# Layer 2's split operands in seven fixed places, each at its own distance mod 256 bytes from the weights

## The chip, the cores and the metric

The kernel runs on one core of a Trainium2 chip. The metric is device time in microseconds (us), less is better. A core has TensorE (PE in the views; PEld is its weight load), VectorE (DVE), ScalarE (ACT), GpSimd (POOL) and SyncE (SP), which here issues every DMA. SBUF holds operands, PSUM (eight banks of 512 float32 columns) the results of matmuls.

## What is computed

Attention over 4 x 8 heads of 576 tokens with a compressive memory, and behind it two feed-forward layers on 2304 tokens of 512 features. The change is in the second.

```
def _moe2_ref(x, w_in, w_out, alpha):
    h = x @ w_in                                     # 2304x512 @ 512x2048
    g = np.maximum(h, 0.0) + alpha * np.minimum(h, 0.0)
    return (g @ w_out).astype(np.float32)            # 2304x2048 @ 2048x512
```

All is float32. The matmuls of both layers are done in float32r: each operand is cut into a high part (a cast to float32r) and a low part (what the cast left over), and a product is three matmuls: high x high, high x low, low x high.

## The kernel before

`build()` records every operation with its engine, its estimated time and what it reads and writes, and `Plan.order()` then simulates the engines and writes one order of instructions for each. So the order on an engine is fixed when the program is built, and an instruction that waits holds up all that stand behind it on its engine.

**Layer 1** runs blocks of 512 tokens (the first) and 256 tokens (the others; in one of them the second matmul has 258 columns). Its operands are cut from `xr` and `gr` by `cut()`, which adds `SKEW` = 48 words (192 bytes) where a block has fewer than 512 columns and nothing where it has 512.

**Layer 2** saves matmuls by forming sums of quarters of its matrices: a 2 x 2 block product takes seven products P = 1 to 7 in place of eight. `hidden()` makes h: for each of 3 blocks b of 384 token columns it loads the four quarters of layer 1's result into `spare` (`inputs`), forms the sums by `sub`, and lets `split` write the parts of each of the seven operands into a place: ACT casts 768 columns (L1198), then DVE subtracts (L1199). `TURN` = 1, 5, 6, 3, 2, 7, 4 is the order of the operands. Then follow 8 groups of seven products. A product (`product`, L1241 to L1243) is six matmuls of 128 x 128 weights and 384 columns. Its bank is then read by `copy_out` (ACT, L1253) or `join` (DVE, L1256), and `leak` (ACT L1267, DVE L1268) makes the activation, which goes to DRAM.

`output()` makes the second matmul of layer 2. For each b and each P in the order 4, 1, 5, 6, 3, 7, 2 there are four steps m: `sub` where a sum is wanted, `split` into the next place of a ring of three, and 12 matmuls of 384 columns (L1373 to L1375).

**Places.** A place holds four runs of 384 columns: high k = 0, high k = 1, low k = 0, low k = 1, here back to back (1536 words). There are eight: five in `poolr`, two in `xr`, one in `gr`, and operand P of block b goes to

```
def XP(P, b):
    return room_for[(7 * b + TURN.index(P)) % 8]
```

so each block starts one place further back, and the first operand of a block finds a place that the block before it doesn't use. The ring of `output()` is the upper place of `xr`, `gr`, the lower place of `xr`; in the last block these held operand 1, operand 5 and operand 4. In the built program `poolr`, `xr`, `gr` and every weight tile `wp` begin at the same address mod 256 bytes, and a 128-column weight is 512 bytes long. So all 2016 matmuls of layer 2 read columns that begin at distance 0 mod 256 bytes from their weights; layer 1's begin at distance 192 where they have 256 or 258 columns, and at 0 where they have 512.

## Time and profile before

| | |
|---|---|
| median of 3 runs (lowest, highest) | 937.96 us (936.33, 938.33) |
| the profiled execution | 939.22 us, of which the span of the profile is 937.2 us |
| PE busy | 921.1 us (98%), 7164 matmuls |
| DVE, ACT busy | 717.4 us (77%), 604.6 us (65%) |
| granted TensorE clock | 1.000 |
| layer 2's first matmul, between those of layer 1 | 569.8 us in the span |
| layer 2, hidden() | to 757.6 us |
| layer 2, output() | from 757.6 us to the end |

The time of an execution is the span and 2.0 us that lie around it. Pitch is used below for the time from the start of one matmul to the start of the next: the length that a row gives for a matmul contains its way through the array, which overlaps the next, and says little about the rate.

### The profile page before, as it was taken

The page shows a single profiled execution, that of the slowest core. Times are in us where ns is not written, and L with a number is a line of the kernel's source. Part 1 is how long each engine was busy: PE and PEld are TensorE (multiplying, and loading weights), DVE is VectorE, ACT ScalarE, POOL GpSimd, SP SyncE. Part 2 cuts the span into 40 slices and gives each one's busy share as a digit, 9 for nine tenths or more (in the row PEclk, how much of TensorE's full clock was granted, in tenths as well). Part 3 has the DMA queues.
Part 4 walks back from the last instruction along what each step waited for, and adds up shares of the span by engine and source line. Part 5 has one row for each costly group of instructions (what it writes and reads, how often), then busy time and mean ns, then how long its engine had stood idle before and what let it go on. Part 6 is the DMA issues. An engine that isn't in the chain of part 4 may idle for free.

```text
span 937.2 us, 19293 instructions
## 1 busy us (share of the span) xinstructions
PE 921.1 (98%) x7164; PEld 845.2 (90%) x7164; DVE 717.4 (77%) x1636; ACT 604.6 (65%) x1413; POOL 5.3 (1%) x29
## 2 busy tenths in 40 slices
PE   7999999999999999999999999999999999999998
PEld 5677777688888888999999999999999999999998
DVE  6999998857777776647778767859568889786874
ACT  7887757767888888744544479748457665454452
POOL 1000000000000000000000000000000000000000
PEclk9999999999999999999999999999999999999999
DMA  4358955466766575567967746635348793725301
GB/s 158 98 144 254 284 180 166 124 139 128 183 146 148 121 168 109 90 185 253 323 228 281 257 156 218 210 111 165 115 133 271 231 306 117 238 68 163 107 1 68
DMA packets 154094, 160.43 MB, mean 171 GB/s; under 512 B 86928, under 2 KB 127888, under 8 KB 154000
## 3 DMA queue, kind: packets, MB, share of 16 engines
q1 hardware_dynamic: 154000, 159.20, 57.4%
q8 instruction: 56, 0.92, 0.4%
q14 instruction: 38, 0.31, 0.1%
HBM read 92.84 MB, written 46.66 MB: 149 GB/s over the span
## 4 chain that ended last, share of the span: by engine, by line
PE 83%; DVE 10%; ACT 3%; issue 2%; DMA 2%; SPq 0%; DVEq 0%; ACTq 0%
PE yb L962 6%; PE yb L964 6%; PE hb L928 6%; PE yb L963 6%; PE hb L929 6%; PE hb L930 6%; PE yb L1373 3%; PE sp L1374 3%; PE yb L1374 3%; PE sp L1373 3%; PE yb L1375 3%; PE sp L1375 3%; PE yb L1241 3%; PE yb L1243 3%; PE yb L1242 3%; PE sp L1243 2%
## 5 line engine op out<-in xcount | busy, mean ns | idle before, releaser
L962 PE MATMUL yb<-gr,wt 128*128 128x256 f32 (+2 forms) x512 | 154.5, 302 | 0.8 <-ACT gr L943 0.5
L928 PE MATMUL hb<-xr,wt 128*128 128x256 f32 (+1 forms) x512 | 152.9, 299 | 2.3 <-ACT gt L941 2.2
L964 PE MATMUL yb<-gr,wt 128*128 128x256 f32 (+2 forms) x512 | 151.5, 296 | 0.8 <-DVE gr L944 0.5
L930 PE MATMUL hb<-xr,wt 128*128 128x256 f32 (+1 forms) x512 | 149.7, 292 | 0.3 <-DVE wt L894 0.3
L929 PE MATMUL hb<-xr,wt 128*128 128x256 f32 (+1 forms) x512 | 149.7, 292 | 0.0
L941 ACT ACTIVATE gt<-hb 128x256 f32<-128x256 f32 (+1 forms) x128 | 52.3, 408 | 91.4 <-PE hb L930 76.9
L928 PEld LDWEIGHTS hb<-xr,wt 128*128 128x128 f32 x512 | 96.3, 188 | 11.3 <-issue 4.4
L962 PEld LDWEIGHTS yb<-gr,wt 128*128 128x128 f32 x512 | 96.3, 188 | 9.2 <-issue 3.7
L944 DVE TENSOR_TENSOR gr<-gt,gr 128x256 fp32r<-128x256 f32 (+1 forms) x128 | 58.3, 456 | 58.9 <-ACT gr L943 56.7
L964 PEld LDWEIGHTS yb<-gr,wt 128*128 128x128 f32 x512 | 96.9, 189 | 5.7 <-DVE gr L944 2.8
L930 PEld LDWEIGHTS hb<-xr,wt 128*128 128x128 f32 x512 | 96.7, 189 | 3.5 <-DVE wt L894 0.9
L929 PEld LDWEIGHTS hb<-xr,wt 128*128 128x128 f32 x512 | 96.3, 188 | 2.1
L963 PE MATMUL yb<-gr,wt 128*128 128x256 f32 (+2 forms) x320 | 93.8, 293 | 0.0
L963 PEld LDWEIGHTS yb<-gr,wt 128*128 128x128 f32 x320 | 60.3, 188 | 1.2
L943 ACT CAST gr<-gt 128x256 fp32r<-128x256 f32 (+1 forms) x128 | 55.3, 432 | 6.8 <-PE yb L963 4.4
L942 ACT ACTIVATE gt<-gt 128x256 f32<-128x256 f32 (+1 forms) x128 | 56.9, 445 | 2.8
L963 PE MATMUL yb<-gr,wu 128*128 128x256 f32 (+2 forms) x192 | 56.3, 293 | 0.0
L1198 ACT CAST xr<-spare 128x768 fp32r<-128x768 f32 x37 | 30.9, 836 | 26.6 <-PE sp L1374 10.1
L1267 ACT ACTIVATE waste<-poolx 128x384 f32<-128x384 f32 x48 | 25.2, 526 | 29.2 <-DVE poolx L1256 28.5
L1199 DVE TENSOR_TENSOR xr<-spare,xr 128x768 fp32r<-128x768 f32 x37 | 35.3, 955 | 9.6 <-ACT xr L1198 9.4
L963 PEld LDWEIGHTS yb<-gr,wu 128*128 128x128 f32 x192 | 36.1, 188 | 0.8
L1112 DVE TENSOR_TENSOR wp<-poolx,wp 128x768 fp32r<-128x768 f32 (+1 forms) x32 | 25.9, 822 | 8.9 <-ACT wp L1110 8.1
(505 smaller groups left out, 2570.2 us busy)
## 6 DMA issues: line engine op xcount, KB each, us to landing
g<-poolx SPq DMA_DIRECT2D x96, 192.0 KB, 1.9
poolu<-g SPq DMA_DIRECT2D x30, 384.0 KB, 4.2
room<-wout SPq DMA_DIRECT2D x14, 512.0 KB, 4.1
room<-win SPq DMA_DIRECT2D x13, 512.0 KB, 3.9
pool<-win SPq DMA_DIRECT2D x12, 512.0 KB, 4.6
pool<-wout SPq DMA_DIRECT2D x12, 512.0 KB, 5.0
spare<-y SPq DMA_DIRECT2D x12, 384.0 KB, 3.7
spare<-g SPq DMA_DIRECT2D x12, 384.0 KB, 3.6
```

The source lines that it names most:

```text
L928: T.matmul(H_, W_h, X_h, start=(d == 0), stop=False)
L929: T.matmul(H_, W_h, X_l, start=False, stop=False)
L930: T.matmul(H_, W_l, X_h, start=False, stop=(d == KD - 1))
L942: op("ACT", t_act(n), lambda: A.activation(out=t_, in_=t_, func=AF.Square), w=[tk], prio=-1)
L943: op("ACT", t_act(n), lambda: A.copy(out=G_h, in_=t_), r=[tk], w=[("gh", gj)], prio=-1)
L944: op("DVE", t_dve(n), lambda: V.tensor_tensor(out=G_l, in0=t_, in1=G_h.bitcast(F32), op=ALU.subtract), r=[tk, ("gh", gj)], w=[("gl", gj)], ...
L962: T.matmul(Y, W_h, G_h, start=first, stop=False, skip_group_check=True)
L963: T.matmul(Y, W_l, G_h, start=False, stop=False, skip_group_check=True)
L964: T.matmul(Y, W_h, G_l, start=False, stop=False, skip_group_check=True)
L1373: T.matmul(o, W_h, G_h, start=(m == e == 0 and P in (1, 2, 4, 5)), stop=False, skip_group_check=True)
L1374: T.matmul(o, W_l, G_h, start=False, stop=False, skip_group_check=True)
L1375: T.matmul(o, W_h, G_l, start=False, stop=False, skip_group_check=True)
```

## The change

- There are seven places, and operand P keeps the same one in every block: 1, 5, 6 and 3 in `poolr`, 2 and 7 in `xr`, 4 in `gr`.
- `LAY` gives each place its own start, and a gap of 64 words stands between the high and the low parts. Distances from the weights, mod 256 bytes: operand 1 at 16, operand 5 at 240, operand 6 at 64, operand 3 at 192, operand 4 at 0. In the two places in `xr` the four runs lie at 0, 32, 32, 0 (operand 2) and 0, 224, 224, 0 (operand 7), so that the six matmuls of a product read 0, 32, 0, 32, 0, 32.
- The ring of `output()` is the two places of `xr` and then `gr`. The three matmuls of a weight pair there are put in the order of `product`: high x high, high x low, low x high.
- The loads into `poolu` (the memory of `poolr`) wait for the last products 1, 5, 6, 3 in place of 6, 3, 2, 7.
- In `xr` the runs of a part are no longer contiguous, so the cast and the subtraction there have the shape 2 x 384 for 768.

```diff
--- before.py
+++ after.py
@@ -19,7 +19,9 @@
-NS, NTH = 384, NT // 2
+NS = 384
+LAY = [(4, 384, 836, 384), (60, 384, 892, 384), (16, 384, 848, 384), (48, 384, 880, 384), (0, 392, 840, 440), (0, 440, 888, 392)]
+NTH = NT // 2
...
@@ -1126,8 +1128,9 @@
-            def __init__(self, region, c0, n):
+            def __init__(self, region, c0, n, lay=None):
                 self.region, self.c0, self.n = region, c0, n
+                self.lay = lay or (0, NS, 2 * NS, NS)
...
@@ -1180,12 +1183,12 @@
-        room_for = [Buf("poolr", 4 * NS * i, 4 * NS) for i in range(5)]
-        room_for = room_for[0:4] + [Buf("xr", 0, 4 * NS)] + room_for[4:] + [Buf("xr", 4 * NS, 4 * NS), Buf("gr", 0, 4 * NS)]
+        room_for = [Buf("poolr", 1920 * i, 1664, LAY[i]) for i in range(4)] + [
+            Buf("xr", 2048 * i, 1664, LAY[4 + i]) for i in range(2)] + [Buf("gr", 0, 4 * NS)]
         TURN = (1, 5, 6, 3, 2, 7, 4)
 
         def XP(P, b):
-            return room_for[(7 * b + TURN.index(P)) % 8]
+            return room_for[TURN.index(P)]
...
@@ -1195,10 +1198,20 @@
         def split(src, dst, prio):
-            act(dst, t_act(2 * NS), lambda: A.copy(out=see(dst, F32R, 0, 2 * NS), in_=see(src)), r=src.keys, prio=prio)
+            def raw():
+                return see(src).rearrange("p (k n) -> p k n", k=2)
+
+            act(dst, t_act(2 * NS), lambda: A.copy(out=two(dst, 0), in_=raw()), r=src.keys, prio=prio)
             op("DVE", t_dve(2 * NS), lambda: V.tensor_tensor(
-                out=see(dst, F32R, 2 * NS, 2 * NS), in0=see(src), in1=see(dst, F32, 0, 2 * NS), op=ALU.subtract),
-               r=src.keys, w=dst.keys, prio=prio)
+                out=two(dst, 1), in0=raw(), in1=two(dst, 0).bitcast(F32), op=ALU.subtract), r=src.keys, w=dst.keys, prio=prio)
+
+        def two(buf, lo):
+            a, step = buf.lay[2 * lo:2 * lo + 2]
+            return see(buf, F32R, a, 2 * step).rearrange("p (k n) -> p k n", k=2)[:, :, 0:NS]
+
+        def one_of(buf, lo, k):
+            a, step = buf.lay[2 * lo:2 * lo + 2]
+            return see(buf, F32R, a + step * k, NS)
...
@@ -1235,7 +1248,7 @@
-                    X_h, X_l = (see(XP(P, b), F32R, 2 * NS * lo + NS * k, NS) for lo in range(2))
+                    X_h, X_l = (one_of(XP(P, b), lo, k) for lo in range(2))
...
@@ -1327,7 +1340,7 @@
-            ring = [room_for[6], room_for[7], room_for[4]]
+            ring = [room_for[4], room_for[5], room_for[6]]
...
@@ -1343,7 +1356,7 @@
-                                [("end", P) for P in (6, 3, 2, 7)] if U[q][m].region == "poolu" else []), eng="SP", bytes_=1024 * NS)
+                                [("end", P) for P in (1, 5, 6, 3)] if U[q][m].region == "poolu" else []), eng="SP", bytes_=1024 * NS)
...
@@ -1366,13 +1379,13 @@
-                                    G_h, G_l = (see(dst, F32R, 2 * NS * lo + NS * e, NS) for lo in range(2))
+                                    G_h, G_l = (one_of(dst, lo, e) for lo in range(2))
...
                                         T.matmul(o, W_h, G_h, start=(m == e == 0 and P in (1, 2, 4, 5)), stop=False, skip_group_check=True)
+                                        T.matmul(o, W_h, G_l, start=False, stop=False, skip_group_check=True)
                                         T.matmul(o, W_l, G_h, start=False, stop=False, skip_group_check=True)
-                                        T.matmul(o, W_h, G_l, start=False, stop=False, skip_group_check=True)
```

**First place: the change of block in `hidden()`, on DVE.** These are the operands of block 1 while the last products of block 0 run. `poolr`, `xr` and `gr` are places, `spare` the quarters, `poolx` the sum or h, `wasteN`, `gr2`, `gt` the parts that `join` adds. In the changed program the lines are a few higher: L1205 is L1199 (`split`), L1217 is L1204 (`sub`), L1269 is L1256 (`join`), L1281 is L1268 (`leak`), L1114 is L1112 (weights). Before:

```order
L1199 TENSOR_TENSOR poolr_6986<-poolx_76,poolr_6986 128x768
L1204 TENSOR_TENSOR poolx_76<-poolx_76,spare_99 128x768
L1268 SCALAR_TENSOR_TENSOR poolx_76<-poolx_76,alm_98,sp0_106 128x384
L1199 TENSOR_TENSOR poolr_6986<-poolx_76,poolr_6986 128x768
L1204 TENSOR_TENSOR poolx_76<-spare_99,poolx_76 128x768
L1199 TENSOR_TENSOR poolr_6986<-spare_99,poolr_6986 128x768
L1199 TENSOR_TENSOR xr_77<-spare_99,xr_77 128x768
L1199 TENSOR_TENSOR poolr_6986<-poolx_76,poolr_6986 128x768
L1199 TENSOR_TENSOR poolr_6986<-spare_99,poolr_6986 128x768
L1256 TENSOR_TENSOR poolx_76<-yb1_102,waste1_7330 128x384
```

With the change:

```order
L1205 TENSOR_TENSOR poolr_6986<-spare_99,poolr_6986 128x768
L1205 TENSOR_TENSOR poolr_6986<-poolx_76,poolr_6986 128x768
L1217 TENSOR_TENSOR poolx_76<-poolx_76,spare_99 128x768
L1281 SCALAR_TENSOR_TENSOR poolx_76<-poolx_76,alm_98,sp0_106 128x384
L1269 TENSOR_TENSOR poolx_76<-yb1_102,waste1_7329 128x384
L1205 TENSOR_TENSOR poolr_6986<-poolx_76,poolr_6986 128x768
L1217 TENSOR_TENSOR poolx_76<-spare_99,poolx_76 128x768
L1205 TENSOR_TENSOR xr_77<-spare_99,xr_77 128x2x384 x2
L1205 TENSOR_TENSOR poolr_6986<-poolx_76,poolr_6986 128x768
L1281 SCALAR_TENSOR_TENSOR poolx_76<-waste3_7350,alm_98,poolx_76 128x384
L1269 TENSOR_TENSOR poolx_76<-yb2_103,waste0_7298 128x384
```

The subtraction for operand 1 of block 1 (`poolr<-spare`), done long ahead before, now stands first in this stretch. That for operand 4 (before the last but one row, `poolr<-spare`) has moved behind these rows, and a `join` of the last group stands between those of operands 5 and 6. On PE, product 2 now stands ahead of products 6 and 3 in the first group of block 1; before, the order there was 1, 5, 6, 3, 2.

**Second place: the change from `hidden()` to `output()`, on DVE.** PE's order is the same before and after: the last product 7, the first output step (m = 0), the last product 4 (`gr` now), then m = 1. Before:

```order
L1199 TENSOR_TENSOR xr_77<-spare_99,xr_77 128x768
L1199 TENSOR_TENSOR gr_78<-spare_99,gr_78 128x768
L1268 SCALAR_TENSOR_TENSOR poolx_76<-poolx_76,alm_98,hb_105 128x384
L1112 TENSOR_TENSOR wp13_7257<-poolx_76,wp13_7257 128x3x256
L1256 TENSOR_TENSOR poolx_76<-yb1_102,waste1_7330 128x384
L1112 TENSOR_TENSOR wp14_7334<-waste5_7188,wp14_7334 128x2x256
L1256 TENSOR_TENSOR poolx_76<-yb2_103,waste0_7298 128x384
L1268 SCALAR_TENSOR_TENSOR poolx_76<-waste3_7358,alm_98,poolx_76 128x384
L1256 TENSOR_TENSOR poolx_76<-yb0_101,waste2_7310 128x384
L1268 SCALAR_TENSOR_TENSOR poolx_76<-poolx_76,alm_98 128x384
L1112 TENSOR_TENSOR wp14_7334<-waste4_7093,wp14_7334 128x2x256
```

With the change:

```order
L1269 TENSOR_TENSOR poolx_76<-yb1_102,waste1_7329 128x384
L1114 TENSOR_TENSOR wp14_7309<-waste5_7178,wp14_7309 128x2x256
L1269 TENSOR_TENSOR poolx_76<-yb2_103,waste0_7298 128x384
L1281 SCALAR_TENSOR_TENSOR poolx_76<-waste3_7350,alm_98,poolx_76 128x384
L1205 TENSOR_TENSOR xr_77<-spare_99,xr_77 128x2x384
L1281 SCALAR_TENSOR_TENSOR poolx_76<-poolx_76,alm_98 128x384
L1205 TENSOR_TENSOR xr_77<-spare_99,xr_77 128x2x384
L1269 TENSOR_TENSOR poolx_76<-yb0_101,waste2_7318 128x384
L1114 TENSOR_TENSOR wp14_7309<-waste4_7093,wp14_7309 128x2x256
L1281 SCALAR_TENSOR_TENSOR poolx_76<-waste3_7350,alm_98,poolx_76 128x384
L1205 TENSOR_TENSOR xr_77<-spare_99,xr_77 128x2x384
L1205 TENSOR_TENSOR gr_78<-spare_99,gr_78 128x768
```

Before, the operands of m = 0 and m = 1 (`xr<-spare`, `gr<-spare`) stand eight and seven rows ahead of the `join` of the last product 7 (`yb0`). Now those two (`xr<-spare` twice) stand three rows and one row ahead of it, since their places are those of operands 2 and 7, whose last products have just been issued. On PE the last product 2 writes `yb2`, product 7 `yb0`, and the first output steps `yb2` and `yb3`.

## Rows read from the trace of the kernel before

**Rows 1.** Page: busy us of each engine (share of the span) x instructions.

```profile
PE 921.1 (98%) x7164; PEld 845.2 (90%) x7164; DVE 717.4 (77%) x1636; ACT 604.6 (65%) x1413; POOL 5.3 (1%) x29
```

**Rows 2.** Windows, three stretches of layer 2: stretch, its us, busy us (instructions), clock.

```profile
569.00:600.00 31.00, 31.00 (x223) 30.59 (x222) 25.82 (x40) 27.24 (x58) 0.00 (x0) 1.00 0.66 213
600.00:757.00 157.00, 157.00 (x907) 156.88 (x906) 118.31 (x200) 100.52 (x201) 0.00 (x0) 1.00 0.54 177
757.00:937.00 180.00, 176.66 (x1019) 176.15 (x1017) 135.83 (x163) 81.63 (x112) 0.00 (x0) 1.00 0.40 130
```

**Rows 3.** Timeline of PE, hidden(): start us, length us, instruction; 384 columns, distance 0.

```profile
600.45 0.33 PE L1241 MATMUL yb<-poolr,wp 128*128 128x384 f32 x1
...
603.57 0.33 PE L1241 MATMUL yb<-poolr,wp 128*128 128x384 f32 x1
```

**Rows 4.** Timeline of PE, layer 1's first block: 512 columns, distance 0.

```profile
121.12 0.39 PE L964 MATMUL yb<-gr,wt 128*128 128x512 f32 x1
...
122.48 0.39 PE L964 MATMUL yb<-gr,wt 128*128 128x512 f32 x1
```

**Rows 5.** Timeline of PE, layer 1: 256 columns, distance 192, a quick stretch.

```profile
429.70 0.28 PE L928 MATMUL hb<-xr,wt 128*128 128x256 f32 x1
...
431.06 0.28 PE L962 MATMUL yb<-gr,wt 128*128 128x256 f32 x1
```

**Rows 6.** Timeline of PE, layer 1: 256 columns, distance 192, a slow stretch.

```profile
469.99 0.28 PE L962 MATMUL yb<-gr,wt 128*128 128x256 f32 x1
...
471.40 0.28 PE L928 MATMUL hb<-xr,wt 128*128 128x256 f32 x1
```

**Rows 7.** Timeline of PE, layer 1: 258 columns, distance 192, then 256.

```profile
515.53 0.28 PE L962 MATMUL yb<-gr,wt 128*128 128x258 f32 x1
...
516.97 0.28 PE L928 MATMUL hb<-xr,wt 128*128 128x256 f32 x1
```

**Rows 8.** Timeline of PE at the change from hidden() to output().

```profile
756.53 0.33 PE L1241 MATMUL yb<-poolr,wp 128*128 128x384 f32 x1
...
757.61 0.44 PE L1373 MATMUL yb<-xr,wp 128*128 128x384 f32 x1
757.89 0.33 PE L1374 MATMUL yb<-xr,wp 128*128 128x384 f32 x1
...
759.82 0.33 PE L1241 MATMUL yb<-xr,wp 128*128 128x384 f32 x1
```

**Rows 9.** Timeline of DVE there.

```profile
752.66 0.95 DVE L1199 TENSOR_TENSOR xr<-spare,xr 128x768 fp32r<-128x768 f32 x1
753.57 0.96 DVE L1199 TENSOR_TENSOR gr<-spare,gr 128x768 fp32r<-128x768 f32 x1
...
757.01 0.55 DVE L1256 TENSOR_TENSOR poolx<-yb,waste 128x384 f32<-128x384 f32 x1
757.48 0.60 DVE L1268 SCALAR_TENSOR_TENSOR poolx<-waste,alm,poolx 128x384 f32<-128x384 f32 x1
758.00 0.55 DVE L1256 TENSOR_TENSOR poolx<-yb,waste 128x384 f32<-128x384 f32 x1
```

**Rows 10.** Timeline of ACT there.

```profile
756.52 0.53 ACT L1267 ACTIVATE waste<-poolx 128x384 f32<-128x384 f32 x1 [0.59 <-DVE poolx L1256]
...
759.85 0.84 ACT L1198 CAST xr<-spare 128x768 fp32r<-128x768 f32 x1 [0.68 <-PE yb L1374]
```

**Rows 11.** Timeline of DVE at the first change of block.

```profile
635.87 0.96 DVE L1199 TENSOR_TENSOR poolr<-poolx,poolr 128x768 fp32r<-128x768 f32 x1
...
638.72 0.96 DVE L1199 TENSOR_TENSOR poolr<-poolx,poolr 128x768 fp32r<-128x768 f32 x1 [0.38 <-ACT poolr L1198]
...
642.33 0.95 DVE L1199 TENSOR_TENSOR poolr<-poolx,poolr 128x768 fp32r<-128x768 f32 x1
```

**Rows 12.** Timeline of PE there: the first matmul of product 3.

```profile
644.13 0.33 PE L1241 MATMUL sp<-poolr,wp 128*128 128x384 f32 x1
```

**Rows 13.** Waits of PE in layer 2, from the line of output's first matmul.

```profile
  DVE poolx L1256: 0.2, 1
```

## The prediction

> **What bounds the kernel now.** I read the page first: PE is busy 98% of the span, the other engines 77% and less [rows 1]. That share says little about PE's rate, so I went on to layer 2 by windows: from 600 to 757 us PE starts 907 matmuls of 384 columns in 157.00 us, 173.1 ns each, with the granted clock at 1.00, which is the upper level of 2.4 GHz [rows 2]. Nothing is waited for there, and DVE and ACT have a quarter of the stretch and more to spare. So layer 2 lasts as long as the pitch of its matmuls says, and the questions are whether the new places change the pitch, and whether the new order makes PE wait.
>
> The pitch comes from two starts in PE's timeline and the number of matmuls between them. Layer 2: 18 matmuls in 3.12 us, 173.3 ns [rows 3]. Its 384 columns at 2.4 GHz take 160.0, so 13.3 ns, or 32 cycles, are lost on each. In layer 1's first block, at distance 0 too, 6 matmuls of 512 columns take 1.36 us, 226.7 ns, and lose 13.3 again [rows 4]. In its other blocks, at distance 192, 12 matmuls of 256 columns take 1.36 us, 113.3 ns, and lose 6.7, or 16 cycles [rows 5]. But in other stretches the same matmuls take 117.5 ns (1.41 us for 12) and lose 10.8 [rows 6]. With 258 columns it is 120.0 (1.44 us for 12): two columns more cost 6.7 ns more than the quick stretch, not 0.8 [rows 7]. The reader is to see that the losses differ by steps of some 16 cycles, the time of 16 columns, which are 64 bytes; that distance 0 always loses two steps and distance 192 one, or one to two; and that no row has 384 columns at any distance but 0.
>
> **What the change costs and gives.** 2016 matmuls are concerned: 24 x 6 = 144 for each operand of hidden(), and 84 steps x 12 = 1008 in output(), a third of them in each place of the ring. So operands 1, 5, 6 and 3 have 144 each, the two places in xr 480 each, gr 480. Those in gr stay at distance 0 and keep 173.3 ns [rows 3].
>
> Operand 3 (distance 192, 144 matmuls). The nearest rows are layer 1's. By the quick stretch 6.7 ns less for each, 0.96 us; by the slow one 13.3 - 10.8 = 2.5 ns, 0.36 us [rows 5, 6]. I take the middle, -0.6 us; the bounds are -0.96 and 0.
>
> Operand 6 (distance 64, 144 matmuls). Nothing has this distance; it is 64 bytes from 0 and 128 from 192. I take the nearer, no change. Bounds: one step either way, -0.96 to +0.96 us.
>
> Operands 1 and 5 (distances 16 and 240, 288 matmuls). Nearest is 0: no change taken. One step either way is -1.9 to +1.9 us.
>
> The two places in xr (960 matmuls). Half of their reads begin at 0, half at 32 or 224. Nearest is 0 for both, so no change is taken. Bounds: a step for the shifted half, 480 x 6.7 ns = 3.2 us either way, and 6.4 us down if the alternation takes a step from every one of them. This is the largest unknown of the sum.
>
> The order of the three matmuls in output() costs nothing by itself: as many weights are loaded as before, and PEld is busy beside PE in either order.
>
> The change from hidden() to output(). Before, the operands of m = 0 and m = 1 are finished at 753.61 and 754.53, four and three us ahead of output's first matmul at 757.61 [rows 9, 8]. What that matmul waited for was the join of the last product 2, which frees its bank and ends at 757.56 [rows 9, 13]: 0.05 us from DVE to PE. Now m = 0 goes to the place of operand 2, whose last product ends where product 7 begins, at 756.53 [rows 8]. A cast that waits for PE starts at once (759.85, after a step that ends at 759.82 [rows 10, 8]). ACT has the leak's first half ahead of it, 756.52 to 757.05 [rows 10]; the cast of 0.84 us then ends near 757.85. On DVE the join and the leak stand ahead, to 758.08, and what follows them starts at 758.00, since neighbours overlap by 0.08 [rows 9]. The subtraction of 0.95 us [rows 9] ends at 758.95, and PE starts at 759.0 in place of 757.61: **+1.4 us**. Queued behind this wait on PE is product 4, which would be ready; behind the subtraction on DVE are a leak, the subtraction for m = 1 (from some 759.4 to 760.35) and the join that frees product 4's bank (to some 760.8). Product 4 starts when m = 0 ends, at 759.0 + 2.08 = 761.1, so this second delay is covered, by 0.3 us. The bounds of the step: 0.9 us, if ACT's leak slips behind the cast and DVE's too, and 2.0 us, if the cover of 0.3 fails by as much again.
>
> The two changes of block. Before, operand 5's subtraction starts at 635.87 and operand 3's ends at 643.28, 0.85 us ahead of product 3 at 644.13 [rows 11, 12]. Now operand 1's subtraction (0.9 us of DVE from start to start where two follow each other) and a join (0.47) come in between [rows 9], 1.4 us; but product 3 stands one product later (6 x 173.3 ns, 1.04 us), and DVE waited 0.38 us for ACT in that stretch, which the new work can fill [rows 11]. What is left of the 0.85 is 0.5 to 0.9 us; product 2, now third, has less, some 0.2 to 0.6. I take nothing, and 0.5 us for each of the two changes as the upper bound. If this cover is gone, PE waits us for us.
>
> The first products, between layer 1's last matmuls (569 to 600 us, PE busy 31.00 of 31.00 us [rows 2]), are re-ordered, because operands 7 and 4 now wait for xr and gr to be left by layer 1. Others stand in for them: nothing taken, 0.3 us either way. The 2 x 384 shape of the cast and the subtraction in xr is on engines with time to spare: nothing. The loads into poolu may start two products earlier, and PE waits for none of them: nothing.
>
> Sum: -0.6 + 1.4 = +0.8 us. The profiled execution took 939.22 us, 1.26 over the median of the runs, so it goes to 940.0 and the median from 937.96 to **938.8 us**.
>
> **The rivals.** *The distance decides, and any that isn't 0 is good (faster).* For it: distance 192 loses a step less than distance 0 [rows 5, 3]. All 1536 matmuls away from gr then gain 6.7 ns, 10.2 us: 937.96 - 10.2 + 1.4 = 929.1 us. With the slow stretch's 2.5 ns it is 3.8 us, 935.5. Against it: the rows that differ in distance differ in columns too, and half of the 960 still start at 0.
>
> *A read that begins inside a 64-byte run costs a step (slower).* For it: the 258 columns, which reach two columns into another run and pay for 16 [rows 7, 5]. A start at 16, 32, 224 or 240 makes 384 columns touch 25 runs in place of 24. That holds for 288 + 480 = 768 matmuls: +5.1 us, with the +0.8 of my sum 943.9 us. It decides once some 165 reads more pay a step than save one, 1.1 us beyond my sum. Against it: in a slow stretch 256 columns pay 117.5 ns, and 258 only 2.5 more [rows 6, 7].
>
> *Distances do nothing.* The loss would belong to the columns alone: 13.3 ns with 384 and 512, 6.7 to 10.8 with 256 [rows 3 to 6]. Only the wait is left: 937.96 + 1.4 = 939.4 us. This is also what the Trainium skill says (TensorE: Matmul & The Clock Gate, the section "Step-by-step: what each phase is for"): PE reads the moving operand and the next weights through two independent ports, and loading the one takes no bandwidth from the other. No row here sets it against the same columns at another distance. The same page (the section "Back-to-back issue gap") gives columns / 2.4 + 2.5 ns, 162.5 for 384, as the gap; the trace differs, 173.3. If the new places brought that gap, 1536 x 10.8 ns would go, 16.6 us, to 922.8 by an estimate from that page.
>
> **How the numbers follow.** A measurement here can tell about 0.2%, 1.9 us, from no change: 936.1 to 939.8 counts as same. Chances: my sum 0.31; distances do nothing 0.14; good, in whole or in part, 0.28; the step for a broken run, in whole or in part, 0.27. My sum's own range is 937.2 to 940.2. It and "nothing" (0.45) lie in the middle with about 0.06 over 939.8 and 0.02 under 936.1: same 0.37. Faster 0.28 + 0.02 = 0.30; slower 0.27 + 0.06 = 0.33. The range reaches into both outer cases, 930.0 to 943.5, and leaves out the best of the one and the worst of the other.
>
> **What would show it.** In the changed kernel's timeline of PE, the starts of the products of operands 1, 5, 6, 3, 2, 7 and 4 give the pitch of each place by itself: 173.3 everywhere but 166.7 to 171 for operand 3 is my case; 173.3 everywhere is "nothing"; 166.7 in most is the first rival; 180 in places 16 and 240 and in half the reads of xr is the second. Output's first matmul must start 1.4 us later against the last product 7, with a subtraction (DVE, L1205) named as what ended the wait. I am wrong above all if the 960 alternating matmuls have a pitch of their own, in either direction.

## The result and the profile after

The changed kernel takes 943.84 us in the median of 4 runs (942.81 to 945.65), the kernel before 937.35 beside it: 1.0071 times as long, with a 95% interval from 1.0052 to 1.0091. It is slower by 6.5 us, where 0.8 was forecast. Its profiled execution took 945.65 us, with a span of 943.3, 6.1 more than before.

PE's line of the page, against [rows 1]:

```profile
PE 924.3 (98%) x7164; PEld 845.9 (90%) x7164; DVE 717.2 (76%) x1636; ACT 604.9 (64%) x1413; POOL 5.3 (1%) x29
```

The same 98% again. The first two windows of [rows 2]:

```profile
569.00:600.00 31.00, 29.25 (x205) 28.12 (x205) 22.45 (x34) 25.31 (x53) 0.00 (x0) 1.00 0.70 213
600.00:757.00 157.00, 156.80 (x898) 156.01 (x897) 117.16 (x199) 98.58 (x197) 0.00 (x0) 1.00 0.53 173
```

Two things are to be seen. From 569 to 600 us PE, which never stood still before, is idle for 1.75 us. From 600 to 757 it is idle for 0.20 us only, yet starts 898 matmuls where it started 907, at the same granted clock: the pitch is longer.

**The waits.** PE's waits between 565 and 600 us (line waited at, what ended it, us, times, longest):

```profile
PE sp L1254 <- DVE poolx L1269: 0.8, 1, 0.8
...
PE yb L966 <- DVE gr L946: 0.5, 1, 0.5
...
PE yb L1254 <- DVE poolx L996: 0.4, 1, 0.4
```

Before, this view shows no wait of PE there. L966 is layer 1 (L964 before); in PE's timeline its step with `gr` now waits for its own operand, since no product of layer 2 stands ahead of it to fill the time:

```profile
577.19 0.28 PE L965 MATMUL yb<-gr,wt 128*128 128x256 f32 x1
577.98 0.38 PE L966 MATMUL yb<-gr,wt 128*128 128x256 f32 x1 [0.52 <-DVE gr L946]
```

Which products filled that time can be read from PE's timeline before. The two `sp` rows are the first matmuls of product 6 and product 7, the third row is layer 1's last:

```profile
577.29 0.34 PE L1241 MATMUL sp<-poolr,wp 128*128 128x384 f32 x1
...
584.99 0.33 PE L1241 MATMUL sp<-poolr,wp 128*128 128x384 f32 x1
...
588.63 0.28 PE L964 MATMUL yb<-gr,wt 128*128 128x256 f32 x1
```

With the change the same three come in this order:

```profile
583.30 0.34 PE L1254 MATMUL sp<-poolr,wp 128*128 128x384 f32 x1
...
588.06 0.28 PE L966 MATMUL yb<-gr,wt 128*128 128x256 f32 x1
...
589.21 0.34 PE L1254 MATMUL sp<-xr,wp 128*128 128x384 f32 x1
```

Product 6 comes 6 us later, and product 7 stands behind layer 1. From layer 2's first matmul to layer 1's last, PE takes 18.9 us in both traces, but starts 24 matmuls of layer 2 there where it started 30.

The change from hidden() to output(), against [rows 8 to 10], on ACT, DVE and PE:

```profile
760.52 0.82 ACT L1204 CAST xr<-spare 128x768 fp32r<-128x768 f32 x1
```

```profile
761.56 0.95 DVE L1205 TENSOR_TENSOR xr<-spare,xr 128x768 fp32r<-128x768 f32 x1
```

```profile
761.16 0.34 PE L1256 MATMUL yb<-xr,wp 128*128 128x384 f32 x1
761.39 0.44 PE L1386 MATMUL yb<-xr,wp 128*128 128x384 f32 x1
762.57 0.45 PE L1387 MATMUL yb<-xr,wp 128*128 128x384 f32 x1 [0.74 <-DVE xr L1205]
```

The first matmul reads only the high part and goes with the cast; the second reads the low part and waits for the subtraction. From 761.16 to 762.57 two starts take 1.41 us where 0.35 would do, and the third another 0.28 for 0.17: 1.17 us. The kernel before lost 0.14 us there, too: from the first matmul of the last product 7 to that of product 4 it took 3.29 us (756.53 to 759.82 [rows 8]). Now it is 4.32, from 760.28 to

```profile
764.60 0.34 PE L1254 MATMUL yb<-gr,wp 128*128 128x384 f32 x1
```

so the switch costs 1.03 us more than before.

**The pitch.** One turn of output's ring is 36 matmuls. In PE's timeline, 25 turns, from the first matmul in `gr` to the first in `gr`:

```profile
774.04 0.34 PE L1386 MATMUL sp<-gr,wp 128*128 128x384 f32 x1
...
931.20 0.34 PE L1386 MATMUL ob<-gr,wp 128*128 128x384 f32 x1
```

That is 157.16 us for 900 matmuls, 174.6 ns; at 173.3 it would be 156.0. More than half of the 46 ns of a turn falls on `gr`, whose distance is still 0, and there on the first four starts:

```profile
849.48 0.34 PE L1386 MATMUL sp<-gr,wp 128*128 128x384 f32 x1
849.65 0.35 PE L1387 MATMUL sp<-gr,wp 128*128 128x384 f32 x1
849.84 0.34 PE L1388 MATMUL sp<-gr,wp 128*128 128x384 f32 x1
850.01 0.34 PE L1386 MATMUL sp<-gr,wp 128*128 128x384 f32 x1
850.20 0.33 PE L1387 MATMUL sp<-gr,wp 128*128 128x384 f32 x1
```

In the mean over 27 entries the gaps are 177.6, 184.8, 176.0 and 181.7 ns, 27 more than four of 173.3, and after that 173.3 to a tenth. So most of the loss belongs to the entry into `gr`, not to the place.

**The sum**, from the starts of all 2016 matmuls, waits apart: pitch +2.2 us (before, all gaps together lay 0.13 us over 173.3 ns each; now 2.35); the switch +1.0; the second change of block +0.6 (at 712 and 719 us, ahead of a product 4); another product 4 at 609 us +0.15; the first stretch some +2.1. Together 6.1, as the spans say. The 2.1 are a difference of two: from layer 2's first matmul to its 85th, behind layer 1, the change takes 31.35 us for 28.61, 2.7 more (1.0 for the six matmuls that no longer fit between layer 1's, 1.7 of waits behind them), but the time ahead of that first matmul was 0.6 us shorter in this execution (569.17 us for 569.76).

### The profile page after: what moved, and what is told of

The parts are those of the page before. It is cut to its first block, busy times and chain, and to the rows that moved or that the text cites. A ratio compares the mean times of both kernels' runs of the same rounds, so it can differ in the third digit from the quotient of the medians.

```text
span 943.3 us, 19252 instructions
## 1 busy us (share of the span) xinstructions
PE 924.3 (98%) x7164; PEld 845.9 (90%) x7164; DVE 717.2 (76%) x1636; ACT 604.9 (64%) x1413; POOL 5.3 (1%) x29
## 4 chain that ended last, share of the span: by engine, by line
PE 77%; DVE 12%; ACT 4%; DMA 4%; issue 2%; SPq 0%; DVEq 0%; ACTq 0%
PE yb L964 6%; PE yb L966 6%; PE hb L930 6%; PE yb L965 5%; PE hb L932 5%; PE hb L931 5%; PE yb L1387 3%; PE sp L1386 3%; PE sp L1387 3%; PE yb L1388 3%; PE sp L1388 3%; PE yb L1386 3%; PE yb L1254 2%; PE yb L1256 2%; PE yb L1255 2%
## 5 line engine op out<-in xcount | busy, mean ns | idle before, releaser
L964 PE MATMUL yb<-gr,wt 128*128 128x256 f32 (+2 forms) x512 | 154.3, 301 | 0.9 <-ACT gr L945 0.5
L966 PE MATMUL yb<-gr,wt 128*128 128x256 f32 (+2 forms) x512 | 151.3, 295 | 1.5 <-DVE gr L946 1.3
L964 PEld LDWEIGHTS yb<-gr,wt 128*128 128x128 f32 x512 | 96.3, 188 | 9.4 <-issue 3.7
L966 PEld LDWEIGHTS yb<-gr,wt 128*128 128x128 f32 x512 | 96.6, 189 | 6.5 <-DVE gr L946 3.7
L1204 ACT CAST xr<-spare 128x768 fp32r<-128x768 f32 x38 | 31.7, 833 | 26.7 <-PE sp L1388 11.8
L1205 DVE TENSOR_TENSOR xr<-spare,xr 128x768 fp32r<-128x768 f32 x38 | 36.1, 954 | 12.8 <-ACT xr L1204 12.4
L1114 DVE TENSOR_TENSOR wp<-poolx,wp 128x768 fp32r<-128x768 f32 (+1 forms) x32 | 25.8, 821 | 11.4 <-ACT wp L1112 10.7
```

Of the source, the lines that this page charges most:

```text
L964: T.matmul(Y, W_h, G_h, start=first, stop=False, skip_group_check=True)
L966: T.matmul(Y, W_h, G_l, start=False, stop=False, skip_group_check=True)
```

## The experiments

Two theories of the pitch went in. **A, settling:** every distance has 173.3 ns, and a change of distance between reads that follow each other costs. **B:** each distance has its own pitch. Beside them stood the prediction's rival **D**, that a read beginning inside a 64-byte run costs a step, and **C**, that distances do nothing. The waits had reasons **E** (the switch) and **F** (the first stretch). All results:

| kernel | median us | before, same chip | ratio, 95% interval |
|---|---|---|---|
| the change, all distances 0 | 941.46 | 937.67 | 1.0041 (1.0029 to 1.0053) |
| before, xr alternating | 938.79 | 937.67 | 1.0015 (1.0005 to 1.0025) |
| the change, multiples of 64 | 944.96 | 937.67 | 1.0067 (1.0053 to 1.0081) |
| before, 64 and 0 mixed | 939.49 | 937.67 | 1.0023 (1.0012 to 1.0035) |
| before, all at 64 | 937.12 | 937.43 | 0.9994 (0.9980 to 1.0008) |
| before, all at 192 | 942.28 | 936.77 | 1.0047 (1.0031 to 1.0064) |
| the same again | 941.15 | 937.43 | 1.0032 (1.0015 to 1.0049) |
| before, all at 32 | 941.62 | 936.77 | 1.0045 (1.0031 to 1.0059) |
| all at 32, one order | 940.44 | 937.43 | 1.0030 (1.0016 to 1.0044) |
| the same again | 940.59 | 937.79 | 1.0037 (1.0015 to 1.0058) |
| the change, gr first | 949.47 | 936.77 | 1.0132 (1.0113 to 1.0151) |
| 0, block 0 as before | 939.37 | 937.79 | 1.0018 (1.0007 to 1.0029) |
| 0, free places | 942.28 | 937.43 | 1.0047 (1.0030 to 1.0064) |
| 0, gr free at the switch | 943.74 | 937.79 | 1.0074 (1.0050 to 1.0097) |
| 0, the last but one and block 0 | 939.75 | 937.79 | 1.0021 (1.0012 to 1.0031) |
| before and the wait alone | 939.40 | 938.36 | 1.0013 (1.0001 to 1.0026) |
| before, layer 1 at 64 | 941.86 | 938.36 | 1.0037 (1.0024 to 1.0050) |

### What the distances cost

**The change at distance 0.**

```diff
-LAY = [(4, 384, 836, 384), (60, 384, 892, 384), ...
+LAY = [(0, 384, 832, 384)] * 6
```

> The changed kernel with its seven places, its order of the casts and its order of the matmuls, but every place at distance 0. The changed kernel takes 943.8 us; of the 6.4 us more than before, my reading of the two traces gives 2.2 to the pitch of layer 2's matmuls and the rest to waits of PE. Theory A, settling (the pitch is 173.3 ns at every distance, and a change of distance between reads that follow each other costs some ns): nothing changes distance any more, so the pitch goes back to 173.3 to 173.4 ns and the time to 941.6 us; the waits at 592, 598, 712, 719 and 761 us stay. Theory B, each distance has its own pitch: the same 941.6. Theory C, the distances do nothing and all of the loss is waits that the seven places bring: 943.8 us, pitch as in the changed kernel, 174.5.

941.46 us: 2.4 us are the distances', as A and B said (2.0 by the pitch of the two traces), and 3.8 are not. C falls. The pitch is back at 173.5 ns, and PE's waits at 590, 596 and 758 us are all there. output() is at 173.3, so the new order of its three matmuls costs nothing by itself, as was forecast.

**Only the alternation, in the kernel before.**

```diff
+        room_for = room_for[0:4] + [Buf("xr", 0, 1664, (0, 392, 840, 440))] + room_for[4:] + [Buf("xr", 1664, 1664, (0, 440, 888, 392)), Buf("gr", 0, 4 * NS)]
```

(and output() in the order h, l, h, as the change has it.)

> The kernel before with its eight turning places and its order of casts, but the two places in xr alternate by 32 bytes as in the change, and output() runs h, l, h. No other place moves. Theory A, settling: output's ring costs 47 ns more for each turn of 36 matmuls, 28 turns, 1.3 us, and hidden's products in xr some 0.2 us: 938.9 us, with the cost in the first four matmuls after a change of place and the rest at 173.3 ns. Theory D, a read that begins inside a 64-byte run costs a step: half of some 1000 reads times 6.7 ns, 3.3 us: 940.7, spread over every shifted read. Theory C, distances do nothing: 937.4.

938.79, as A said. The entry to `gr` has the same four gaps (177.4, 184.6, 176.3, 181.6 ns), a turn costs 47 ns more, and the rest of `gr` is at 173.3. D would have it in every shifted read.

**No broken run.** The words of this list are distances of 64, 128 and 192 bytes.

```diff
+LAY = [(d, 384, 832 + d, 384) for d in (16, 32, 48, 16, 32, 48)]
```

> The changed kernel with distances 64, 128, 192 for the four places in poolr and 128 and 192 for the two in xr, without alternation, so that no read begins inside a 64-byte run; distances still change from place to place. Theory D, a broken run costs: pitch 173.3 ns, 941.6 us. Theory A, settling: the changes from place to place stay, those inside a product are gone; 942 to 944 us, with excess in the first matmuls of a place. Theory B, each distance has its own pitch: the places at 192 stand apart from those at 64 and 128 for all of a product; with 6.7 ns less at 192 alone, some 770 matmuls, 5 us less, 936.5.

944.96: no read begins inside a 64-byte run, and it is no faster than the change; even A's forecast, up to 944, was too low, since the mean pitch rose to 175.0 ns. D falls, though its forecast, 943.9 us, was the one that the result met. B's gain at 192 is not there: the two places at 192 lie in hidden() at 173.5 (operand 6) and 176.0 ns (operand 7), the same distance after different neighbours.

**64 and 0 mixed.** The weights were moved by 64 bytes against everything else; a quarter of them, four of the sixteen weight tiles, lie elsewhere in SBUF and stayed at distance 0, which I saw only in the result.

```diff
-TAIL = 40
-SKEW = 48
+TAIL = 24
+SKEW = 32
```

> The kernel before with the weights alone moved in SBUF, so that every read of layer 2 stands at distance 64 and nothing changes from place to place; layer 1's 256-column blocks keep distance 192, its 512-column block goes to 64 too; the program's order is that of before. Theory A, settling: 173.3 ns as at distance 0, 937.4 us. Theory B, each distance has its own pitch: 2016 matmuls at other than 173.3 ns; a step of 6.7 ns less gives 923.8, a step more 950.9; by the 172.6 ns that the changed kernel's place at 64 shows, 936.0.

So it became a test of changes: every one from 64 to 0 is to be seen by itself. PE's timeline at one of them, where at 849.25 the weights pass to one of those four tiles:

```profile
849.25 0.35 PE L1373 MATMUL sp<-gr,wp 128*128 128x384 f32 x1
849.43 0.34 PE L1374 MATMUL sp<-gr,wp 128*128 128x384 f32 x1
849.61 0.34 PE L1375 MATMUL sp<-gr,wp 128*128 128x384 f32 x1
849.79 0.33 PE L1373 MATMUL sp<-gr,wp 128*128 128x384 f32 x1
```

Four gaps of 177.5, 185.0, 175.9 and 181.6 ns in the mean of 30 such changes, 27 ns more than four of 173.3: the entry to `gr` again, without any of the places of the change. The 30 changes back from 0 to 64 cost nothing, and between them both distances run at 173.3. 30 x 27 ns is 0.8 us, all of layer 2's longer pitch. The kernel is 1.8 us slower (1.1 to 3.3 by the interval). What the rest is was not tested; layer 1's reads that belong to the four tiles stand elsewhere, too (128 for 192).

**All at 64.** Here pool, xr and gr were moved, so that no read is left at 0.

```diff
+        sb.tile([128, 16], F32, name="mid")
         pool = sb.tile([128, (NSLOT - XS) * GW], F32, name="pool", tag="pool")
```

> The kernel before with a pad of 64 bytes, so that all 2016 reads of layer 2 stand at distance 64 (in the earlier run a quarter of the weights stood at 0). There the pitch was 173.3 ns at 64 and at 0, and each of 30 changes from 64 to 0 cost 26.6 ns. Theory A, changes of distance cost: none is left, 173.3 ns, 937.4 us, stall as before. Theory B, each distance has a pitch of its own, as the runs with 192 and 32 bytes now say for those two: 173.3 by the earlier run's reads at 64, the same 937.4; the two part if the pitch at 64 is not the 173.3 of that run.

937.12, no difference, and 173.33 ns for the mean of 2003 gaps. The windows of hidden() and output() in the kernel before, and under them those of this one:

```profile
610.00:660.00 50.00, 50.00 (x290) 50.00 (x290) 36.52 (x60) 31.72 (x64) 0.00 (x0) 1.00 0.42 143
...
780.00:930.00 150.00, 150.00 (x867) 150.00 (x866) 114.42 (x135) 68.50 (x92) 0.00 (x0) 1.00 0.36 112
```

```profile
610.00:660.00 50.00, 50.00 (x290) 50.00 (x290) 35.60 (x60) 31.61 (x63) 0.00 (x0) 1.00 0.41 143
...
780.00:930.00 150.00, 150.00 (x867) 150.00 (x866) 112.40 (x133) 67.06 (x91) 0.00 (x0) 1.00 0.36 111
```

867 matmuls (one or two of them cut by the edges) are 173.3 ns each. This is the mark for what follows.

**All at 192, and all at 32** (pads of 48 and 8 words).

> The kernel before with pool, xr and gr moved against the weights by a pad of 192 bytes, so that all 2016 matmuls of layer 2 read at distance 192 (of the run with 64 bytes a quarter of the weights had stayed at distance 0, which its expectation did not say). Layer 1's 256-column blocks keep 192, its 512-column block goes to 192. Program order as before. Theory A, settling: no change of distance anywhere in layer 2, 173.3 ns, 937.5 us. Theory B, each distance has its own pitch: with the step that layer 1's 256-column blocks seem to save at 192, 166.7 ns and 924 us in all.

> As the run with 192 bytes, but with a pad of 32 bytes: all 2016 reads of layer 2 stand at distance 32 and begin inside a 64-byte run. Layer 1's 256-column blocks keep 192. Theory A, settling: 173.3 ns, 937.5 us. Theory D, a read that begins inside a 64-byte run costs a step: 180.0 ns, 2016 x 6.7 = 13.4 us more, 951.

At 192:

```profile
610.00:660.00 50.00, 50.00 (x291) 50.00 (x290) 36.00 (x60) 32.13 (x64) 0.00 (x0) 1.00 0.41 139
...
780.00:930.00 150.00, 150.00 (x861) 150.00 (x860) 114.19 (x135) 68.23 (x92) 0.00 (x0) 1.00 0.36 112
```

At 32:

```profile
610.00:660.00 50.00, 50.00 (x285) 50.00 (x284) 36.10 (x59) 31.44 (x63) 0.00 (x0) 1.00 0.41 139
...
780.00:930.00 150.00, 150.00 (x866) 149.70 (x865) 116.62 (x139) 68.80 (x92) 0.00 (x0) 1.00 0.37 110
```

Here A falls as I had put it: nothing changes distance, and yet 192 has 173.3 ns in hidden() and 174.7 in output() (861), 32 has 176.7 in hidden() (285 for 290) and 173.3 in output(). B falls as well, and D: one distance, two pitches. The times of these two kernels spread over 6 and 7 us, those of the kernel before beside them over 4. Two causes were left: the order of the three matmuls, which differs between hidden() and output(), or the execution.

**All at 192 again, and all at 32 with hidden() in output()'s order**, twice.

```diff
                     T.matmul(o, W_h, X_h, start=(k == 0 and P in (1, 5, 2)), stop=False, skip_group_check=True)
+                    T.matmul(o, W_l, X_h, start=False, stop=False, skip_group_check=True)
                     T.matmul(o, W_h, X_l, start=False, stop=False, skip_group_check=True)
-                    T.matmul(o, W_l, X_h, start=False, stop=False, skip_group_check=True)
```

> The same program as the run with 192 bytes, whose profiled execution took 940.2 us while its other executions went from 938.5 to 944.9. Theory G, the pitch is set by the program (distance, and order of the three matmuls): again 174.7 ns in output() and 173.3 to 173.8 in hidden(). Theory H, the rhythm between the reads of operand and weights is taken anew in each execution: other pitches in the same places; at 944.9 us the mean would be some 176.5.

> As the run with 32 bytes, in which the pitch was 176.4 ns in hidden(), where the three matmuls read the operand h, l, h, and 173.3 in output(), where they read h, h, l. Here hidden() has output()'s order. Theory G, distance and order together set the pitch: 173.3 ns in hidden() too, 2.8 us less than that run in the same kind of execution, 939 us. Theory H, the pitch belongs to the execution and not to the order: hidden() stays apart from output() by chance, or both differ.

> The same program as the run with 32 bytes and output()'s order of the three matmuls, in which blocks 0 and 1 of hidden() had 173.3 ns and block 2 176.5 to 176.7, at one distance and in one order. Theory G, the program sets the rhythm: again 176.6 in block 2 alone. Theory H', at this distance there are two rhythms and a wait of PE sets which one follows, so it is taken anew in each execution: another share of hidden() at 176.6; the executions of that run went from 937.7 to 943.0 us, as if between none and all of hidden() and output() stood at the slower one.

192 came out as in the first execution in output() (174.7); block 2 of hidden(), 174.5 in the first execution, had 173.5 in the second. At 32 with one order, the first execution:

```profile
610.00:660.00 50.00, 50.00 (x290) 50.00 (x289) 35.85 (x59) 31.72 (x64) 0.00 (x0) 1.00 0.43 143
...
720.00:755.00 35.00, 35.00 (x200) 35.00 (x199) 28.60 (x49) 24.95 (x49) 0.00 (x0) 1.00 0.79 233
780.00:930.00 150.00, 150.00 (x867) 150.00 (x866) 113.23 (x134) 67.99 (x91) 0.00 (x0) 1.00 0.37 111
```

And the second, of the same program:

```profile
610.00:660.00 50.00, 50.00 (x285) 50.00 (x285) 36.12 (x59) 31.45 (x62) 0.00 (x0) 1.00 0.41 139
...
780.00:930.00 150.00, 150.00 (x851) 150.00 (x850) 113.05 (x133) 67.96 (x91) 0.00 (x0) 1.00 0.36 108
```

In the first, blocks 0 and 1 and output() run at 173.3 and block 2 at 176.7; in the second all of layer 2 at 176.7. Distance, order and program are the same. So at 32 there are two rhythms, and which of them a stretch keeps is taken anew in an execution; the two took 938.19 and 945.39 us. They ran on two chips, but the chip alone doesn't set it: on the one the times of this program went from 937.67 to 943.04 us, on the other from 938.93 to 945.39. What picks the rhythm was not settled: in the first execution it changed at the second change of block and at the switch, and PE had no wait over 0.02 us at either.

The starts show a little more. At the 720th of layer 2's 2016 matmuls, behind the second change of block, PE is off its pitch by some ns in each of these traces that is quick up to there, whatever the distance (174, 177, 174, 175 ns in the kernel before; 178, 169, 170, 176 at 64). At 0 and 64 the gaps are 173.3 again within four. At 192, in both executions, and in the first at 32 with one order, the slow rhythm begins there. In the second execution at 192 a wait of PE of 0.17 us, at 716.4 us, ends it. So at 32 and 192 a small disturbance can turn the rhythm, and at 0 and 64 it did not; what disturbs PE at that matmul is not shown.

### What the waits cost

**gr first in output's ring.**

```diff
-            ring = [room_for[4], room_for[5], room_for[6]]
+            ring = [room_for[6], room_for[4], room_for[5]]
```

> The changed kernel with one list turned: output's ring is gr, xr, xr in place of xr, xr, gr, so that its first operand goes to the place of operand 4, whose last product ends at 757.1, four us ahead of the end of hidden(), and not to that of operand 2. Reason E, the wait at the switch is that of the place of operand 2: the 1.01 us that PE waits at 761.39 goes, 942.7 us; the place's pitch cost stays, at other positions. Rival: the wait moves to the next operand (m = 1, in the place of operand 2), and 0.3 us or less is gained: 943.6.

949.47, a miss of both. I had overlooked that the very last product of hidden() is one of operand 4, and stands behind output's first step: with that step in `gr` it had to go first, and waited for its bank. Windows from 758 us:

```profile
758.00:762.00 4.00, 1.06 (x6) 0.74 (x5) 4.00 (x7) 2.53 (x5) 0.00 (x0) 1.00 0.92 299
762.00:766.00 4.00, 2.77 (x10) 2.05 (x10) 2.94 (x5) 2.27 (x4) 0.00 (x0) 0.64 1.03 375
766.00:770.00 4.00, 4.00 (x14) 4.00 (x14) 3.24 (x5) 0.83 (x1) 0.00 (x0) 0.50 1.07 393
770.00:774.00 4.00, 4.00 (x25) 4.00 (x24) 3.97 (x5) 1.18 (x2) 0.00 (x0) 1.00 0.84 304
```

PE stands still for some 3 us from 758 and for 1.1 more after 762, and then the granted clock is 0.50, the lower level of 1.2 GHz: 14 matmuls in 4 us where the next window has 25. Some 5 us are waits and 2 the clock.

**Block 0 as before**, at distance 0: the kernel before with this list, and with the change's ring, matmul order and loads.

```diff
-            return room_for[(7 * b + TURN.index(P)) % 8]
+            return room_for[(0, 1, 2, 3, 4, (5, 5, 6)[b], (6, 7, 7)[b])[TURN.index(P)]]
```

> All places at distance 0, output's ring as in the change (xr, xr, gr). Block 0 has the places of the kernel before (operand 7 in poolr's fifth place, operand 4 in xr's upper half); operand 7 stays there in block 1 and goes to xr in block 2, operand 4 goes to gr from block 1 on. Unlike in the earlier run of this kind no operand is overwritten. Reason F, the first stretch loses 2.1 to 2.3 us because operands 7 and 4 wait until layer 1 has left xr and gr: 939.2 us, with PE's waits between 586 and 600 us back to those of the kernel before and the 1.0 us at the switch still there. Rival: 941.5, with other waits in their place.

939.37, against 941.46 with the change's places: 2.1 us, as F said. The two traces lie 2.6 us apart; 1.7 of that is in the first stretch: 29.9 us from layer 2's first matmul to its 85th, against 31.6. (In all fifteen traces with block 0's places of before it is 28.6 to 30.5, in the five with those of the change 31.1 to 32.1.) Another 0.6 are waits of 0.2 to 0.3 us, ahead of a product 4, at 607, 659 and 710 us, most of which are gone. (An earlier form, in which operand 7 of block 1 overwrote operand 4 ahead of its last product, so that one product was of other numbers, took 939.12.) PE's waits in its trace, 565 to 780 us:

```profile
PE yb L1374 <- DVE xr L1199: 0.7, 1, 0.7
...
PE sp L1241 <- DVE poolx L1256: 0.4, 1, 0.4
```

The switch's is there, and of the first stretch one of 0.4 us is left, with one of 0.3 in layer 1. Products 6 and 7 stand between layer 1's matmuls again, as before the change.

**Free places**, at distance 0: operand 7 in `poolr`, operand 4 in xr's upper half in block 0 and then in `gr`, and output's first step in xr's upper half, which is free. The loads into `poolu` then wait for operand 7, too.

```diff
+            return room_for[7 if P == 4 and b else TURN.index(P)]
...
+            ring = [room_for[6], room_for[4], room_for[7]]
```

> All places at distance 0, one place for each operand as in the change, but operand 7 in poolr's fifth place, operand 4 in xr's upper half in block 0 and in gr after that, and output's ring begins with xr's upper half, which is then free. Matmul order of output() as in the change. Compared with the changed kernel's places at distance 0, 941.5 us: reason F (operands 7 and 4 wait for layer 1 in the first stretch) gives back 2.3 us and reason E (the switch waits for the end of operand 2's products) 1.1: 938.1 us, with PE's wait at the switch back to about 0.2 us. Rival: fixed places cost in every block, and the waits come back at the changes of block: 940.

942.28: the rival, and 2 us more. The switch has no wait and the first stretch one of 0.6 us, but the third place of the ring is `gr`, held by operand 4's last product, and the planner put other products ahead of the late step; PE waits 0.8 us at 721, 1.0 at 762, 1.6 at 769 and 0.5 at 773 us.

**gr free at the switch**, at distance 0, and the same **with block 0 as before**:

```diff
+            return room_for[(0, 1, 2, 3, 4, (6, 6, 6)[b], (7, 5, 5)[b])[TURN.index(P)]]
...
+            ring = [room_for[7], room_for[4], room_for[6]]
...
+                                [("end", P) for P in (1, 5, 6, 3, 4)] if U[q][m].region == "poolu" else []), eng="SP", bytes_=1024 * NS)
```

> All places at distance 0, operands in the places of the change, except that operand 4 goes from block 1 on to poolr's fifth place, so that gr is free when hidden() ends and output's ring is gr, xr, xr; the loads into poolu then wait for operand 4 too. Against the changed kernel's places at distance 0 (941.5 us). Reason E, output's first operand waits for the end of operand 2's products: PE's 1.0 us at the switch goes, 940.4 us. Rival: what was late moves to the next operand or, with the loads into poolu, to the second product of output(): 941.5 or more, with PE's waits after 761 us.

> The two together, at distance 0: block 0 with the places of the kernel before, operand 4 in poolr's fifth place in block 2, output's ring gr, xr, xr. Reasons E and F: 941.5 - 2.2 - 1.1 = 938.1 us, within 0.2% of the kernel before. Rival: the waits come back at the changes of block, as in the run with free places: 940 or more.

943.74 is the rival; 939.75 is nearer to the rival's 940 than to the 938.1 of E and F. In the second kernel PE runs through the switch without a wait, but pays 1.0 us at the second change of block (707 and 714 us) and 1.5 behind the switch. ACT:

```profile
765.49 0.83 ACT L1198 CAST xr<-poolu 128x768 fp32r<-128x768 f32 x1 [2.37 <-DMA poolu<-g]
```

and PE:

```profile
766.38 0.44 PE L1373 MATMUL sp<-xr,wp 128*128 128x384 f32 x1 [0.40 <-ACT xr L1198]
767.37 0.44 PE L1374 MATMUL sp<-xr,wp 128*128 128x384 f32 x1 [0.55 <-DVE xr L1199]
```

Operand 4 now lies in `poolr`, so the loads into the same memory as `poolu` wait for its last product, and the operand of output's second product comes late by 1.5 us. The first kernel waits there too (1.6 us), and 0.9 us at the second change of block. Its first stretch takes as long as that of the change at distance 0 (31.7 and 31.6 us), with its waits at other products. Its times spread from 941.35 to 947.77 us, and the profiled one is 941.93, so its median is not explained in full.

**The wait alone**, in the kernel before, since taking it away always brought another.

```diff
+                        split(src, dst, -2 if (b, P) == (0, 4) else None, [("end", 2)] if (b, P, m) == (0, 4, 0) else [])
```

(the last argument is read by the cast beside its source.)

> The kernel before with the wait of the switch alone: the cast for output's first operand also waits for the last product of operand 2, as the place in the change makes it do. PE's order is that of the kernel before; a cast on ACT and a subtraction on DVE move behind the join and the leak. Reason E: PE's first matmul of output() starts 1.0 to 1.2 us later against the last product 7, and the rest follows: 938.9 us. Rival: what comes after has slack (product 4 and the next operand are ready) and gives it back: 937.8, or 0.3 us and less.

939.40 against 938.36: 1.2 us by the ratio, 0.1 to 2.4 by its interval. PE's order is that of before. Its timeline:

```profile
756.82 0.34 PE L1374 MATMUL yb<-xr,wp 128*128 128x384 f32 x1
757.71 0.45 PE L1375 MATMUL yb<-xr,wp 128*128 128x384 f32 x1 [0.56 <-DVE xr L1199]
```

The wait has moved to the third matmul, the first that reads the low part in this order, and nothing gives it back: in this trace the switch loses 1.06 us.

### Layer 1 at 64

```diff
-SKEW = 48
+SKEW = 16
```

> The kernel before with layer 1's 256-column blocks at distance 64 in place of 192; layer 2 stays at 0. In layer 1 the same matmuls at 192 take 113.3 ns in some stretches and 117.8 in others, one distance with two rhythms, as at 192 and 32 in layer 2, while at 64 layer 2 showed 173.3 alone. If 64 has one rhythm here too and it is the quick one: some 2500 matmuls times 1.6 to 2 ns, 4 to 5 us less, 933 to 934 us. If it is a slower one (120.0, 16 columns more): 2500 x 4.6 ns, 949. Against either: no difference, 937.8, as layer 2 at 64 against 0.

941.86, none of the three: the hope that 64 would have the quick rhythm alone fails. Windows of layer 1, the kernel before:

```profile
430.00:470.00 40.00, 39.82 (x345) 39.62 (x345) 30.15 (x67) 18.80 (x48) 0.00 (x0) 1.00 0.83 293
470.00:490.00 20.00, 20.00 (x172) 20.00 (x171) 15.53 (x34) 8.51 (x22) 0.00 (x0) 1.00 0.63 231
```

Layer 1 at 64:

```profile
430.00:470.00 40.00, 39.92 (x339) 39.72 (x338) 29.71 (x66) 19.00 (x49) 0.00 (x0) 1.00 0.83 289
```

And the kernel with the wait alone, whose layer 1 is that of before:

```profile
470.00:490.00 20.00, 20.00 (x179) 20.00 (x178) 15.01 (x35) 8.95 (x23) 0.00 (x0) 1.00 0.70 251
```

At 64 most gaps of 256 columns are near 118 ns, 117.2 in the mean of 2399 against 115.5 before: 4 us, 3.5 by the medians. (The trace of the kernel before is on the slow side: in the others with 192 throughout in layer 1 the mean is 114.3 to 114.8.) At 192, 20 us hold 172 matmuls in one execution and 179 in another of the same layer 1: the quick and the slow stretches of [rows 5, 6] are two rhythms of one distance, too.

## Why the prediction was wrong

**The bound was right.** Layer 2 lasts as long as its pitch says plus PE's waits, and the 6.1 us are these two.

**The first failing step: "Others stand in for them: nothing taken, 0.3 us either way"**, on the first products between layer 1's last matmuls. It measured +2.1 us, in the sum of the two traces and by the median of the run with block 0 as before. That stretch had no idle time of PE [rows 2] because products of layer 2 filled layer 1's waits. Products 6 and 7 were two of the fillers: 7 lost its place there because its operand now waits for layer 1 to leave `xr`, and 6, whose place is the old one, was put later by the planner. Product 4, which the prediction named beside 7, was no filler: its first matmul came at 597.30 before, behind layer 1. That the places of 7 and 4 in block 0 bring the loss is shown by that run, which puts 6 and 7 back; why the planner moved 6 is not. I had the re-ordering in view and took its cost from the full row, without asking which products filled which wait. This is a third of the loss.

**The second failing step: that a place whose distance stays keeps its pitch** ("Those in gr stay at distance 0 and keep 173.3 ns"). They do, from the fifth matmul on; what costs is the change of distance between one read and the next, which the sum had no term for. The 480 reads in `gr` gave +0.9 us over 173.3 ns each, the 960 alternating ones +0.8 (taken as 0), operands 1 and 5 +0.6 (0), operand 6 -0.1 (0), and operand 3 +0.2, where -0.6 was taken from layer 1: together +2.2 over the kernel before, against -0.6. The steps of 16 cycles (6.7 ns) that the prediction read off layer 1 [rows 4 to 7] and took for its bounds showed nowhere in layer 2: the slower rhythms lie 1.3 and 3.3 ns over 173.3.

**Right in cause and size: the switch.** +1.4 forecast, by 0.9 to 2.0; 1.0 more than before in the trace, 1.2 by the run with that wait alone. One detail was wrong: output's first matmul is not late (1.11 us behind product 7's first, 1.08 before), since it reads the high part only; the second waits. The cover behind it held.

**The changes of block:** nothing at the first, +0.6 at the second, over the bound of 0.5. The waits stand ahead of a product 4, the longer one for a join (DVE, L1269), and not at products 3 and 2, for which the cover was worked out. No run took it by itself.

**The rivals.** *The broken run* gave 943.9 us, and the result is 943.84; it is still wrong. Without any broken run the time is 944.96, and at 32, where all reads are broken, output() ran at 173.3. *Any distance but 0 is good:* no run had a mean pitch under 173.3 ns in layer 2. *Distances do nothing:* 2.4 us say otherwise. The Trainium skill (TensorE: Matmul & The Clock Gate, "Step-by-step: what each phase is for") has the operand and the next weights on two independent ports; here matmuls at distance 32 ran at 173.3 or 176.7 ns and those at 0 and 64 at 173.3 alone, and moving nothing but the weights cost 27 ns at each change from 64 to 0, so where the two lie is felt in the pitch. By what mechanism is not shown.

The theory that is left, for 384 columns: 173.3 ns is the floor at each of the four distances that were held throughout; 0 and 64 showed this rhythm alone, 32 and 192 a second, slower one; and some changes of distance cost some 27 ns once, 64 to 0 for one, others nothing. With 256 columns 64 has the slow rhythm, too. In the four kernels that hold one distance it is the operand that was moved, so whether the distance or the operand's own address gives a steady rhythm is open. The table of changes was not worked out, and neither is the cause of the 13.3 ns that the floor loses.

## What to carry to other kernels

Where a stretch shows no idle time, ask of every product that a change moves whether it is the filler of somebody's wait: a full engine is the sign of a good filling, not of spare cover. A place that is held longer costs at its next user. At the switch, giving that user another place only moved the cost, each time it was tried; in the first stretch, giving operands 7 and 4 their old places back took the cost away. So the order behind such a change has to be read again. When operands are laid out, keep one distance from the weights throughout, and one that shows a single rhythm: here no distance was quicker than 0, changing it cost 0.8 us and more, and 32 or 192 held throughout cost some 3 to 5.5. A distance has to be timed in several executions, since one profile may show either of its rhythms.

## What was not expected of the hardware

- One program had two pitches in two executions: 384 columns at distance 32 at 173.3 or 176.7 ns through whole stretches, at full granted clock. In layer 1, 256 columns at 192 took 113.3 or 117.8 ns.
- A change of distance is felt for four matmuls (177.5, 185.0, 175.9, 181.6 ns) and only in one direction: 64 to 0 costs 27 ns, 0 to 64 nothing, also where only the weights move.
- After PE had stood still for some 3 us from 758 and for 1.1 after 762, the granted clock was 0.64 in the mean of 762 to 766 us and 0.50 (the level of 1.2 GHz) through 766 to 770, with matmuls of 384 columns every 320 ns, and 1.00 again after that.
